# Windowed attention with a softplus feed-forward layer: the softmax weights of chunks 2 to 8 turned by VectorE in squares of 32 and a trip through DRAM

## The chip, the cores and the metric

The kernel runs on one core of one Trainium2 chip. The metric is the device time of one execution in microseconds, as the median of several runs; smaller is better.

## The reference

Eight batches of 576 tokens with eight heads of 64 go through causal attention in a window. Heads 0 to 3 see the last 32 keys, heads 4 to 7 see 32 keys with a step of four. The result, 4608 tokens by 512, goes through a feed-forward layer with softplus:

```python
scores = scale * np.matmul(q, k.transpose(0, 1, 3, 2))
scores = np.where(masks[None, :, :, :], scores, -1000000000.0)
scores = scores - np.max(scores, axis=-1, keepdims=True)
attn = np.exp(scores)
attn = attn / (np.sum(attn, axis=-1, keepdims=True) + 1e-09)
x = matmul(attn, v), heads side by side      # 4608 x 512
h = x @ w_in                                 # 4608 x 2048
g = np.maximum(h, 0.0) + np.log1p(np.exp(-np.abs(h)))
out = g @ w_out                              # 4608 x 512
```

Everything is float32; products are made of high and low parts on TensorE, three matmuls for one.

## The kernel before

The 4608 tokens are cut into nine chunks of 512. Chunks 0 and 1 are opened by an order written out by hand and go through the feed-forward layer first, by 32 slots of one feed-forward tile each. For chunks 2 to 8 (`FIRST` is 2) the first product, x times w_in, is made by seven products of half size in place of eight. That is the main loop at the end of the program: for each chunk eight pairs p of feed-forward tiles, and for each pair seven steps k. A step is `product` (six matmuls of 128x256 into one of two PSUM banks, `h_x` or `h_y`), `aside` (VectorE takes the bank out to `temps` or `hs`, L799 and L801), and then one output part, or two after the seventh step (`outputs`, `late_o`: three matmuls of 128x512 into `o_ps`). The banks alternate, so a product can start only when the bank that was filled two products before has been taken out. After steps 6 and 7 come the softplus of two tiles (three ACT passes L512 to L514, DVE L519, ACT L534, DVE L540).

The attention of a later chunk is spread over this loop by a list of events with due times, counted in feed-forward tiles; `pump(now)` after each step runs whatever is due. For each chunk there are four groups (`Group`, two heads each), and `attend(c, j, when, unit)` gives a group three events:

- `scores` at `when`: 32 matmuls of 64x96 into two banks `s_ps` (`score`), scale and mask on VectorE (L345, twice), the row maximum (L348), eight exponentials on ScalarE (L354), the sum's inverse (L366, L369), and the division of all 128x768 weights `s` on GpSimd (L372). Right after it the q and k of the next group are loaded.
- `turn` two tiles later: sixteen TensorE transposes of 64x96 to 96x64 into two banks `t_ps` (L394) and two ScalarE copies of 96x512 to `pt` (L407), so that keys lie on partitions.
- `values` 0.6 tiles after that: 32 matmuls `a_ps` of `v` with `pt`, and a ScalarE copy to `x_full` (L442), which later feeds the sums and splits of the next chunk's half-size products.

`s_ps`, `t_ps` and `a_ps` share two PSUM banks (`att`). In chunks 2 to 8 there is one buffer each for `s`, `pt`, `k` and `v`, and two for `q`. SyncE's queue issues all loads in the order of the events; w_out tiles (`t<-w_out`) are loaded three tiles ahead. TensorE instructions and transfers by `load_dma` are pinned to program order; much of VectorE's work is placed by the framework's scheduler.

Of the kernel before, what the change touches and what calls it, by code (L numbers as in the profile page):

```python
# [13 lines left out]
F32 = mybir.dt.float32  # L14
# [9 lines left out]
P = 128  # L24
# [5 lines left out]
BLK = 64  # L30
WKEYS = BLK + WIN
NB = CH // BLK
NS = NB // 2
# [8 lines left out]
FIRST = 2  # L42
HALF = CH // 2
NPAIR = NFF // 2
EARLY = 6
ON_POOL = 5
NEG = -1.0e9
# [42 lines left out]
def tile_windowed_attention_softplus_ffn(  # L90
# [11 lines left out]
    nc = tc.nc  # L102

    const = ctx.enter_context(tc.tile_pool(name="const", bufs=1))
    wk = ctx.enter_context(tc.tile_pool(name="wk", bufs=2))
    dpool = ctx.enter_context(tc.tile_pool(name="dec", bufs=3))
    psum = ctx.enter_context(tc.tile_pool(name="psum", bufs=2, space=bass.MemoryType.PSUM))
# [3 lines left out]
    slots, at = [], {0: 0, 1: 0}  # L111
# [12 lines left out]
    def pin(ins):  # L124

        if opening:
            tc.keep_in_program_order(ins)

    def load_dma(engine=None, **kw):
        tc.keep_in_program_order((engine or nc.sync).dma_start(**kw))  # L130
# [55 lines left out]
    def matmul(**kw):  # L186
        tc.keep_in_program_order(nc.tensor.matmul(**kw))  # L187

    def bank(name, tag="att"):
        return psum.tile(  # L190
            [P, CH], F32, name=name, tag=tag, bufs=2 if tag in ("att", "h") else 1
        )
# [8 lines left out]
    def scratch(shape, name, c, pr):  # L201

        if c == 0:
            tag = idle.pop(0)
        elif c == 1:
            tag = turns[name][pr % len(turns[name])]
        else:
            tag = f"q{pr % 2}" if name == "q" else name
        return const.tile(shape, F32, name=name, tag=tag)

    masks, xt = {}, {}
# [11 lines left out]
    def x_tiles(c):  # L223

        if c not in xt:
            xt[c] = [
                [const.tile([P, 2, CH], F32R, name=n, tag=f"{n}{c}{k}") for k in range(2)]
                for n in ("xh", "xl")
            ]
        return xt[c]  # L230
# [3 lines left out]
    def x_half(c, k):  # L234
        if (c, k) not in x_full:
            x_full[c, k] = const.tile([P, 2, CH], F32, name="x_full", tag=f"x_{'ab'[k]}")
        return x_full[c, k]
# [20 lines left out]
    def split(c, name):  # L258
        if name not in blocks:
            blocks[name] = const.tile(  # L260
                [P, 2, 2, HALF], F32R, name=name, tag=HOMES[ORDER.index(name)]
            )
        dst, n = blocks[name], int(name[1:])
        if name[0] == "a":
            src = x_block(c, n // 10 - 1, n % 10 - 1)
        else:
            src = combined[c, (n - 1) // 2][:, (n - 1) % 2]
        nc.scalar.copy(out=dst[:, 0], in_=src)
        nc.vector.tensor_tensor(out=dst[:, 1], in0=src, in1=dst[:, 0].bitcast(F32), op=ALU.subtract)

    class Group:
# [6 lines left out]
        def load_k(self, engine=None):  # L278
            kw = DKW if self.dil else PKW
            self.k = scratch([P, kw], "k", self.c, self.pr)  # L280
            src = kdl[self.c, self.pr - 2] if self.dil else kpl[self.c, self.pr]
            load_dma(engine, out=self.k, in_=src)

        def load_q(self):
            self.q = scratch([P, CH], "q", self.c, self.pr)
            load_dma(out=self.q, in_=qp[self.c, self.pr])
# [5 lines left out]
        def load_v(self):  # L292
            self.v = scratch([P, NB, 2, D], "v", self.c, self.pr)
            load_dma(out=self.v[:WKEYS], in_=vp[self.c, self.pr])
# [91 lines left out]
        def transposes(self):  # L386
# [12 lines left out]
                        )  # L399
            self.pt = scratch([P, 2, CH], "pt", self.c, self.pr)  # L400

        def turned(self, g):
            dst, src = self.pt[:WKEYS, g], self.banks[g][:WKEYS]
            if self.own and g:
                pin(nc.vector.tensor_copy(out=dst, in_=src))
            else:
                pin(nc.scalar.copy(out=dst, in_=src))  # L407

        def turn(self):
            self.transposes()  # L410
            self.turned(0)
            self.turned(1)

        def weighted(self):
            a_ps = bank("a_ps", "o2" if self.own else "att")
            by_class = a_ps.rearrange("p (r i) -> p r i", r=DIL)
            per = BLK // DIL
            for i in range(NS):
                for g in range(2):
                    n = 2 * i + g  # L420
                    for r in range(2):
                        rows = slice(r * D, (r + 1) * D)
                        if self.dil:
                            dst = a_ps[rows, n * BLK : (n + 1) * BLK]
                        else:
                            dst = by_class[rows, :, n * per : (n + 1) * per]
                        matmul(
                            out=dst,
                            lhsT=self.v[:WKEYS, n, r, :],
                            rhs=self.pt[:WKEYS, g, (r * NS + i) * BLK : (r * NS + i + 1) * BLK],  # L430
                            start=True,
                            stop=True,
                        )
            if self.c >= FIRST:
                self.x = x_half(self.c, self.pr // 2)[:, self.pr % 2], None, a_ps
                return
            xh, xl = x_tiles(self.c)
            self.x = *(part[self.pr // 2][:, self.pr % 2] for part in (xh, xl)), a_ps
# [15 lines left out]
    groups = [Group(c, pr) for c in range(NCH) for pr in range(NPR)]  # L454
# [24 lines left out]
    def at(when, part, *what):  # L479
        events.append((when, len(events), part, what))  # L480

    def attend(c, j, when, unit):
        n = c * NPR + j
        at(when, scores, n)
        at(when + 2 * unit, turn, n)
        at(when + 2.6 * unit, values, n)

    def pump(now):
        while events and events[0][0] <= now:
# [50 lines left out]
        pin(nc.vector.tensor_tensor(out=gl, in0=e, in1=gh.bitcast(F32), op=ALU.subtract))  # L540
        ready[i] = gh, gl

    dram = ctx.enter_context(tc.tile_pool(name="dram", bufs=1, space=bass.MemoryType.DRAM))
    kept = dram.tile([2, NKT, P, CH], F32, name="kept")
    w_out = dram.tile([NFF, P, 2, DM], F32, name="w_out")
    o_ps = {}
# [91 lines left out]
    for word in OPENING.split():  # L638
        name = word[:3] if word[0] == "D" and word[1] != "l" else word.rstrip("0123456789_")
# [15 lines left out]
    def weight_sum(p, j):  # L655

        parts = wt[2 * p + j, 0].bitcast(F32)
        if p < EARLY:
            sums[p, j] = dpool.tile([P, 2, HALF], F32, name="b", tag="a")
# [8 lines left out]
    def weight_13(p):  # L668
        shape = dict(shape=[P, 2, HALF], dtype=F32, name="t")
        d = diffs[p] = dpool.tile(**shape, tag="a") if p < EARLY else const.tile(**shape, tag="x_d")  # L670
        one, two = sums[p, 0], sums[p, 1]
# [16 lines left out]
    def second(p):  # L688

        q = min(p, NPAIR - 2)  # L690
        return [rests[q][:, p - q, part] for part in range(2)]

    def weight_split_24(p):
        if p < NPAIR - 1:
            rests[p] = const.tile([P, 2, 2, HALF], F32R, name="t2", tag=f"w{2 * p + 1}_1")
        parted(*second(p), sums[p, 1][:, 1])
        b12 = wt[2 * p + 1, 0]
        parted(b12[:, 0, :HALF], b12[:, 1, :HALF], sums[p, 0][:, 1])
# [44 lines left out]
    for ff in range(NFF):  # L743
        at(17.2 + 0.5 * ff, keep_w_out, ff)
    for j in range(NPR):
        attend(FIRST, j, 12 + 3.6 * j, 1)
    for n in range(4):
        at(26 + 0.2 * n, combine, FIRST, n)
    for k in range(4):
        at(27.6 + 0.4 * k, split, FIRST, ORDER[k])  # L750
    for p in range(NPAIR):
        at(20.5 + 1.9 * p if p < EARLY else 36.5 + 3 * (p - EARLY), convert, p)
    for c in range(FIRST + 1, NCH):
        base = 2 * NFF + (c - 1 - FIRST) * NFF
        for j in range(NPR):
            attend(c, j, base + 3.5 * j + (0.6 if c == FIRST + 1 else -0.4), 1)
        for n in range(4):
            at(base + 13.7 + 0.1 * n, combine, c, n)
    events.sort(key=lambda e: e[:2])
# [43 lines left out]
    def late_softplus(u):  # L803
        i = len(slots) + u
        tiles[i] = hs.pop(u)
        activated(i)
        softplus(i)
        g_high(i)
        g_low(i)
# [52 lines left out]
    between = {0: (1, 1, 1, 1, 0, 1, 1), 1: (1, 1, 0, 0, 1, 1, 2)}  # L862
    for n, (c, p) in enumerate((c, p) for c in range(FIRST, NCH) for p in range(NPAIR)):
        u = 2 * n
        for k, (x, weights, b, first, to, temp) in enumerate(steps):
# [5 lines left out]
            if k > 4:  # L871
                late_softplus(u + k - 5)
            if p == NPAIR - 1 and c + 1 < NCH:
                split(c + 1, x)
# [6 lines left out]
    for half in range(2):  # L881
        ob = const.tile([P, NKT, HALF], F32, name="pt", tag=("pt", "v")[half])
        for m in range(NKT):
# [9 lines left out]
            elif m % 2:  # L893
                nc.sync.dma_start(
                    out=out[(m - 1) * P : (m + 1) * P, cols].rearrange("(m p) n -> p m n", p=P),
                    in_=ob[:, m - 1 : m + 1],
# [116 lines left out]
```

## Time and profile before

| | us |
|---|---|
| median of 3 runs | 918.48 |
| lowest and highest run | 916.78, 920.76 |
| the profiled execution's own time | 918.32 |
| span in its profile | 916.5 |
| TensorE busy | 897.8 (98%) |
| VectorE busy | 610.8 (67%) |
| ScalarE busy | 574.1 (63%) |
| GpSimd busy | 62.6 (7%) |

The span is the time from the first to the last instruction of the profiled execution; 1.8 us of its time lie around it. An engine's share is an average over stages, and a matmul's listed duration is longer than the distance to the next one, because matmuls overlap in the array. So the cost of a block of matmuls is read from the distance of the starts around it and not from its durations. The granted TensorE clock is 0.996 of full speed over the span.

### The profile page before, as it was taken

To read this page: it belongs to the slowest core of one execution; us is meant where nothing else is said; L and a number is where in the kernel's file an instruction comes from. 1 tells how busy PE (TensorE), PEld (TensorE's weight loads), DVE (VectorE), ACT (ScalarE), POOL (GpSimd) and SP (SyncE) were. 2 spreads that over 40 slices of the span, in tenths; PEclk is the share of its full clock that TensorE was granted. 3 is DMA by queue.
4 is the path that set the end of the run, shared out by engine and by line. 5 is a ranking of instruction groups with operands and counts; after the bars stand their busy time and mean duration, and the time that the engine had idled before them with its cause. 6 is when DMAs were issued, how large, how long until landed. Compare 5 with 4: busy or idle time off the path is not lost.

```text
span 916.5 us, 19113 instructions
## 1 busy us (share of the span) xinstructions
PE 897.8 (98%) x7426; PEld 756.9 (83%) x7426; DVE 610.8 (67%) x1214; ACT 574.1 (63%) x1404; POOL 62.6 (7%) x46
## 2 busy tenths in 40 slices
PE   7899999999999999999999999999999999999998
PEld 4567877778878888888888888888888888898987
DVE  3899995997685575557655665557556765575444
ACT  5676687776565676666666576567655766654443
POOL 1320000000001000000000000000000000000000
PEclk8999999999999999999999999999999999999999
DMA  9979323225234335343443344333534353324323
GB/s 291 312 244 398 130 87 129 85 81 161 96 122 135 125 125 182 136 137 115 167 150 135 107 148 164 129 134 117 175 136 135 121 176 118 110 93 144 109 93 116
DMA packets 62971, 134.45 MB, mean 147 GB/s; under 512 B 7072, under 2 KB 9248, under 8 KB 62880
## 3 DMA queue, kind: packets, MB, share of 16 engines
q1 hardware_dynamic: 62304, 132.15, 41.8%
q8 instruction: 59, 0.97, 0.4%
q10 hardware_dynamic: 576, 1.07, 0.4%
q14 instruction: 32, 0.26, 0.1%
HBM read 113.27 MB, written 19.92 MB: 145 GB/s over the span
## 4 chain that ended last, share of the span: by engine, by line
PE 87%; DVE 8%; ACT 2%; DMA 1%; issue 1%; POOL 0%; ACTq 0%; DVEq 0%; POOLq 0%
PE o_ps L187 40%; PE h_x L187 18%; PE h_y L187 14%; PE h_ps L187 6%; PE a_ps L187 4%; PE s_ps L187 3%; PE t_ps L394 2%; ACT s L354 1%; DVE a L160 1%; DVE a L165 1%; DVE a L151 1%; DMA k<-kpl 1%; DVE e L519 1%; DVE a L155 1%; DVE gl L540 1%
## 5 line engine op out<-in xcount | busy, mean ns | idle before, releaser
L187 PE MATMUL o_ps<-gh,t 128*128 128x512 f32 (+1 forms) x904 | 341.6, 391 | 0.0
L187 PEld LDWEIGHTS o_ps<-gh,t 128*128 128x128 f32 x904 | 169.7, 188 | 21.3
L187 PE MATMUL o_ps<-gl,t 128*128 128x512 f32 (+1 forms) x452 | 178.2, 394 | 0.3 <-DVE gl L540 0.3
L512 ACT ACTIVATE e<-hs 128x512 f32<-128x512 f32 x112 | 69.1, 627 | 88.8 <-DVE hs L801 87.7
L354 ACT ACTIVATE s<-s,nm 128x96 f32<-128x96 f32 x224 | 80.9, 363 | 65.8 <-DVE nm L348 65.4
L519 DVE SCALAR_TENSOR_TENSOR e<-hs,e 128x512 f32<-128x512 f32 x112 | 79.5, 711 | 54.7 <-ACT e L514 54.7
L534 ACT CAST gh<-e 128x512 fp32r<-128x512 f32 x134 | 82.5, 617 | 42.7 <-DVE e L519 37.8
L540 DVE TENSOR_TENSOR gl<-e,gh 128x512 fp32r<-128x512 f32 x144 | 98.5, 694 | 9.1 <-ACT gh L534 8.8
L372 POOL TENSOR_TENSOR s<-s,ri 128x768 f32<-128x768 f32 x36 | 55.3, 1535 | 720.2 <-DVE ri L369 312.2
L187 PEld LDWEIGHTS h_x<-a,parts 128*128 128x128 f32 x672 | 94.7, 189 | 11.2 <-DVE hs L801 2.0
L187 PE MATMUL h_y<-s,t 128*128 128x256 f32 x672 | 101.6, 287 | 0.5 <-DVE temps L801 0.5
L187 PEld LDWEIGHTS h_y<-s,t 128*128 128x128 f32 x672 | 92.2, 188 | 10.7 <-DVE temps L801 0.9
L187 PE MATMUL h_x<-a,parts 128*128 128x256 f32 x672 | 98.5, 282 | 0.0
L801 DVE TENSOR_TENSOR hs<-h_x,temps 128x256 f32<-128x256 f32 x112 | 47.3, 422 | 66.4 <-PE h_x L187 66.0
L513 ACT ACTIVATE e<-e 128x512 f32<-128x512 f32 x144 | 88.8, 626 | 2.3
L514 ACT ACTIVATE e<-e 128x512 f32<-128x512 f32 x144 | 88.9, 626 | 2.1
L187 PEld LDWEIGHTS o_ps<-gl,t 128*128 128x128 f32 x452 | 86.0, 190 | 3.7 <-DVE gl L540 0.9
L187 PE MATMUL o_ps<-gh,parts 128*128 128x512 f32 x256 | 88.1, 395 | 0.0
L187 PE MATMUL h_ps<-xh,parts 128*128 128x512 f32 x256 | 87.0, 396 | 1.1 <-ACT xh L442 1.1
L801 DVE TENSOR_TENSOR temps<-h_y,temps 128x256 f32<-128x256 f32 x112 | 47.2, 422 | 25.7 <-PE h_y L187 23.8
L187 PEld LDWEIGHTS h_ps<-xh,parts 128*128 128x128 f32 x256 | 48.0, 188 | 12.4 <-ACT xh L442 1.6
L187 PEld LDWEIGHTS o_ps<-gh,parts 128*128 128x128 f32 x256 | 48.1, 188 | 10.4
(80 smaller groups left out, 1291.5 us busy)
## 6 DMA issues: line engine op xcount, KB each, us to landing
t<-w_out SPq DMA_DIRECT2D x224, 256.0 KB, 2.9
raw<-w SPq DMA_DIRECT2D x32, 512.0 KB, 10.2
v<-vp SPq DMA_DIRECT2D x36, 384.0 KB, 3.4
q<-qp SPq DMA_DIRECT2D x36, 256.0 KB, 3.8
w_out<-parts SPq DMA_DIRECT2D x16, 512.0 KB, 3.2
out_t<-ob SPq DMA_DIRECT2D x32, 256.0 KB, 2.1
k<-kdl SPq DMA_DIRECT2D x17, 320.0 KB, 4.0
k<-kpl SPq DMA_DIRECT2D x16, 272.0 KB, 3.2
```

What stands on the lines that cost most here:

```text
L151: pin(nc.vector.tensor_scalar(out=a, in0=a, scalar1=W_MIN, scalar2=W_MAX, op0=ALU.max, op1=ALU.min))
L187: tc.keep_in_program_order(nc.tensor.matmul(**kw))
L354: pin(nc.scalar.activation(out=self.blocks[:, t], in_=src, func=AF.Exp, bias=self.nm[:, t : t + 1], scale=1.0 / 8.0 if self.masked else 1. ...
L372: pin(nc.gpsimd.tensor_tensor(out=self.blocks, in0=self.blocks, in1=self.ri.unsqueeze(2).to_broadcast([P, NB, WKEYS]), op=ALU.mult,))
L394: nc.tensor.transpose(out=banks[g][:WKEYS, (r * NS + i) * BLK : (r * NS + i + 1) * BLK], in_=self.s[rows, k0 : k0 + WKEYS], identity=ident ...
L512: pin(nc.scalar.activation(out=e, in_=tiles[i], func=AF.Abs))
L513: pin(nc.scalar.activation(out=e, in_=e, func=AF.Exp, scale=-1.0))
L514: pin(nc.scalar.activation(out=e, in_=e, func=AF.Ln, bias=1.0))
L519: pin(nc.vector.scalar_tensor_tensor(out=e, in0=tiles.pop(i), scalar=0.0, in1=e, op0=ALU.max, op1=ALU.add))
L534: nc.scalar.copy(out=gh, in_=ready[i])
L540: pin(nc.vector.tensor_tensor(out=gl, in0=e, in1=gh.bitcast(F32), op=ALU.subtract))
L801: nc.vector.tensor_tensor(out=dst, in0=src, in1=temps[:, temp], op=ALU.add)
```

## The change

For chunks 2 to 8 the sixteen transposes and two copies of a group go. In their place VectorE turns `s` in one instruction, each square of 32x32 within its 32 partitions (`turn_squares`); the result (128x768, buffer `q1`) is written to DRAM in one transfer (`send_squares`), and three transfers, one for each 32 keys, read it back into `pt` (`fetch_squares`), 1 KB runs, 128 for each transfer. `values` reads `pt` in two runs of 32. The three of `attend` become five events: scores, turn, send, bring, values. Scores of chunks 4 to 8 are due 1.1 tiles earlier than before, and values 4.5 tiles after their scores in place of 2.6; since scores are 3.5 tiles apart, values now stand behind the scores of the next group. `q` has one buffer (`q0`) in these chunks, since `q1` holds the squares.

```diff
+        def turn_squares(self):
+
+            squares = const.tile([P, WKEYS // SQ, NB, SQ], F32, name="squares", tag="q1")
+            nc.vector.transpose(out=squares, in_=self.blocks.rearrange("p t (b k) -> p b t k", k=SQ))
+            self.squares = squares
+
+        def send_squares(self):
+            self.sent = dram.tile([P, WKEYS // SQ, NB * SQ], F32, name="turned", bufs=2)
+            load_dma(out=self.sent, in_=self.squares.rearrange("p b t n -> p b (t n)"))
+
+        def fetch_squares(self):
+            self.pt = scratch([P, P // SQ, NB, SQ], "pt", self.c, self.pr)
+            for b in range(WKEYS // SQ):
+                load_dma(
+                    out=self.pt[b * SQ : (b + 1) * SQ].rearrange("k q t n -> k q (t n)"),
+                    in_=self.sent[:, b].rearrange("(q k) n -> k q n", k=SQ),
+                )
+
+        def weights_of(self, g, t):
+            if self.c >= FIRST:
+                return self.pt[:WKEYS, 2 * g : 2 * g + 2, t]
+            return self.pt[:WKEYS, g, t * BLK : (t + 1) * BLK]
...
         def turn(self):
+            if self.c >= FIRST:
+                self.turn_squares()
+                return
             self.transposes()
...
-    def attend(c, j, when, unit):
+    def attend(c, j, when, lags):
         n = c * NPR + j
-        at(when, scores, n)
-        at(when + 2 * unit, turn, n)
-        at(when + 2.6 * unit, values, n)
+        for lag, part in zip((0,) + lags, (scores, turn, send, bring, values)):
+            at(when + lag, part, n)
...
-        attend(FIRST, j, 12 + 3.6 * j, 1)
+        attend(FIRST, j, 10.8 + 3.5 * j, (0.5, 2.8, 3.2, 4.5))
...
-            attend(c, j, base + 3.5 * j + (0.6 if c == FIRST + 1 else -0.4), 1)
+            attend(c, j, base + (3.73 * j - 2.1 if c == FIRST + 1 else 3.5 * j - 1.5), (0.5, 2.25, 2.65, 4.5))
```

TensorE, program before: a group's turn, in a stretch of the main loop (`h_x` and `h_y` are products, `o_ps` output parts).

```order
L187 MATMUL h_y<-a_2771,parts 128x256 x6
L187 MATMUL o_ps_2992<-gh,t_2604 128x512
L187 MATMUL o_ps_2992<-gl,t_2604 128x512
L187 MATMUL o_ps_2992<-gh,t_2695 128x512
L394 MATMUL t_ps<-consts,s 96x64 x16
L187 MATMUL h_x<-s_2774,parts 128x256 x6
```

In the changed program (its line numbers are two higher here, 32 higher in the main loop) no row of TensorE has `t_ps` in chunks 2 to 8, and product follows output part directly at these places.

VectorE, program before: the turn from one chunk to the next, where the finished output tiles are copied to `ob`.

```order
L801 TENSOR_TENSOR hs<-h_x,temps 128x256
L519 SCALAR_TENSOR_TENSOR e<-hs,e 128x512
L799 COPY temps<-h_x 128x256
L835 COPY ob<-o_ps_4220 128x512
L540 TENSOR_TENSOR gl<-e,gh 128x512
L519 SCALAR_TENSOR_TENSOR e<-hs,e 128x512
L801 TENSOR_TENSOR temps<-h_y,temps 128x256
L540 TENSOR_TENSOR gl<-e,gh 128x512
L799 COPY hs<-h_x 128x256
L835 COPY ob<-o_ps_4222 128x512
L801 TENSOR_TENSOR temps<-h_y,temps 128x256
L345 SCALAR_TENSOR_TENSOR s<-s_ps,mask 128x384 x2
```

VectorE, changed program, the same turn:

```order
L833 TENSOR_TENSOR hs<-h_x,temps 128x256
L552 SCALAR_TENSOR_TENSOR e<-hs,e 128x512 x2
L347 SCALAR_TENSOR_TENSOR s<-s_ps,mask 128x384 x2
L573 TENSOR_TENSOR gl<-e,gh 128x512
L831 COPY temps<-h_x 128x256
L573 TENSOR_TENSOR gl<-e,gh 128x512
L867 COPY ob<-o_ps_4105 128x512
L350 TENSOR_REDUCE nm<-s 128x8
L833 TENSOR_TENSOR temps<-h_y,temps 128x256
L831 COPY hs<-h_x 128x256
```

The scores of the chunk's second group now stand right behind step 7 of the first pair, so their mask, one `gl`, and later the maximum and a copy to `ob` have come ahead of the first two bank copies of the next pair. This order stands at five turns (the second groups of chunks 4 to 8).

SyncE's queue, changed program, one group's transfers among the loads of w_out:

```order
L132 DMA turned<-squares 128x768
L132 DMA t_2552<-w_out 128x512
L132 DMA t_2683<-w_out 128x512
L132 DMA pt<-turned 32x4x256 x3
L132 DMA t_2069<-w_out 128x512
L132 DMA t_2247<-w_out 128x512
L132 DMA q<-qp 128x512
```

Before, this queue held only loads here; the write and the three reads are new, each with its own place among them.

## Rows read from the trace of the kernel before

**Rows 1.** Busy time by stage: us, then busy us of each engine, clock, DMA share, GB/s.

```profile
100.00:200.00 100.00, 99.10 (x675) 79.47 (x674) 88.15 (x168) 75.75 (x178) 6.47 (x4) 1.00 0.27 98
400.00:520.00 120.00, 120.00 (x1059) 104.34 (x1059) 73.73 (x150) 73.66 (x184) 7.35 (x5) 1.00 0.41 138
```

**Rows 2.** Waits of TensorE: who waited for whom, us in total, times, longest.

```profile
PE t_ps L394 <- POOL s L372: 0.9, 1, 0.9
...
PE h_x L187 <- DVE hs L799: 0.7, 1, 0.7
```

**Rows 3.** Instructions on the tile t_ps: duration in ns, min, median, max.

```profile
L394 PE MATMUL t_ps<-consts,s x576: 216/216/340, 15.2 to 798.5; 64*96 64x64 f32 x192
L407 ACT COPY pt<-t_ps x68: 558/583/607, 18.6 to 799.2; 96x512 f32<-96x512 f32 x68
```

**Rows 4.** Timeline of TensorE around one turn: start us, duration us.

```profile
318.37 0.40 PE L187 MATMUL o_ps<-gh,t 128*128 128x512 f32 x1
...
319.16 0.65 PE L394 MATMUL t_ps<-consts,s 64*96 64x64 f32 x16
319.75 0.98 PE L187 MATMUL h_x<-s,t 128*128 128x256 f32 x6
320.56 0.40 PE L187 MATMUL o_ps<-gh,t 128*128 128x512 f32 x1
...
321.26 0.87 PE L187 MATMUL h_y<-a,parts 128*128 128x256 f32 x6
321.97 0.40 PE L187 MATMUL o_ps<-gh,t 128*128 128x512 f32 x1
```

**Rows 5.** Groups of VectorE instructions by shape: busy us, mean ns.

```profile
L348 DVE TENSOR_REDUCE nm<-s 128x8 f32<-128x768 f32 x28 | 26.4, 943 | 0.0
...
L155 DVE TENSOR_SCALAR a<-a 128x512 int32<-128x512 int32 x32 | 14.3, 456 | 0.3
...
L366 DVE TENSOR_SCALAR sm<-sm 128x8 f32<-128x8 f32 x36 | 6.0, 167 | 15.3 <-ACT s L354 15.3
```

**Rows 6.** Timeline of all engines around one group's scores.

```profile
396.39 0.87 PE L187 MATMUL h_x<-s,parts 128*128 128x256 f32 x6
...
397.29 0.42 DVE L801 TENSOR_TENSOR hs<-h_x,temps 128x256 f32<-128x256 f32 x1 [0.97 <-PE h_x L187]
...
398.94 0.69 DVE L519 SCALAR_TENSOR_TENSOR e<-hs,e 128x512 f32<-128x512 f32 x1 [1.22 <-ACT e L514]
...
399.98 0.89 PE L187 MATMUL s_ps<-k,q 64*64 64x96 f32 x32
...
400.12 0.69 DVE L519 SCALAR_TENSOR_TENSOR e<-hs,e 128x512 f32<-128x512 f32 x1 [0.16 <-ACT e L514]
400.73 0.68 DVE L540 TENSOR_TENSOR gl<-e,gh 128x512 fp32r<-128x512 f32 x1
...
400.80 0.98 PE L187 MATMUL h_y<-s,t 128*128 128x256 f32 x6
...
401.33 1.02 DVE L345 SCALAR_TENSOR_TENSOR s<-s_ps,mask 128x384 f32<-128x384 f32 x2
...
401.62 0.39 PE L187 MATMUL o_ps<-gh,t 128*128 128x512 f32 x1
...
402.26 0.68 DVE L540 TENSOR_TENSOR gl<-e,gh 128x512 fp32r<-128x512 f32 x1
...
402.86 0.42 DVE L801 TENSOR_TENSOR temps<-h_y,temps 128x256 f32<-128x256 f32 x1
...
403.19 0.94 DVE L348 TENSOR_REDUCE nm<-s 128x8 f32<-128x768 f32 x1
...
404.05 0.41 DVE L799 COPY hs<-h_x 128x256 f32<-128x256 f32 x1
...
408.12 1.47 POOL L372 TENSOR_TENSOR s<-s,ri 128x768 f32<-128x768 f32 x1 [21.04 <-DVE ri L369]
```

**Rows 7.** Transfers: KB each, median us from issue to landing.

```profile
v<-vp SPq DMA_DIRECT2D x36, 384.0 KB, 3.4
...
w_out<-parts SPq DMA_DIRECT2D x16, 512.0 KB, 3.2
```

More of the change, by code (lines that the diff above doesn't have):

```diff
@@ L44 @@
 NPAIR = NFF // 2
+SQ = 32
 EARLY = 6
@@ L104, in tile_windowed_attention_softplus_ffn @@
     const = ctx.enter_context(tc.tile_pool(name="const", bufs=1))
+    dram = ctx.enter_context(tc.tile_pool(name="dram", bufs=1, space=bass.MemoryType.DRAM))
     wk = ctx.enter_context(tc.tile_pool(name="wk", bufs=2))
@@ L207, in scratch @@
         else:
-            tag = f"q{pr % 2}" if name == "q" else name
+            tag = "q0" if name == "q" else name
         return const.tile(shape, F32, name=name, tag=tag)
@@ L429, in weighted @@
                             lhsT=self.v[:WKEYS, n, r, :],
-                            rhs=self.pt[:WKEYS, g, (r * NS + i) * BLK : (r * NS + i + 1) * BLK],
+                            rhs=self.weights_of(g, r * NS + i),
                             start=True,
@@ L480, in at, with send, bring @@
         events.append((when, len(events), part, what))
-    def attend(c, j, when, unit):
+    def send(n):
+        groups[n].send_squares()
+    def bring(n):
+        groups[n].fetch_squares()
+    def attend(c, j, when, lags):
         n = c * NPR + j
-        at(when, scores, n)
-        at(when + 2 * unit, turn, n)
-        at(when + 2.6 * unit, values, n)
+        for lag, part in zip((0,) + lags, (scores, turn, send, bring, values)):
+            at(when + lag, part, n)
     def pump(now):
@@ L541, in g_low @@
         ready[i] = gh, gl
-    dram = ctx.enter_context(tc.tile_pool(name="dram", bufs=1, space=bass.MemoryType.DRAM))
     kept = dram.tile([2, NKT, P, CH], F32, name="kept")
```

## The prediction

> **What bounds the kernel now.** I read the table by stage first. [...] The loop is a TensorE loop with spare time on every other engine, but the spare time before each single hand-over is small, and that is where this change must be read. The stage of chunk 2's attention (100 to 200 us) is tighter: TensorE 99, VectorE 88 of 100 [rows 1].
>
> **What goes.** 576 transposes in sixteens are 36 groups [rows 3]; eight belong to chunks 0 and 1 and stay, 28 go. A duration of 216 ns each is no cost, since they overlap. The cost is read from starts [rows 4]. Without a block, a product follows the start of an output part after 0.70 us (320.56 to 321.26) and the next output part follows after 0.71 (to 321.97). With the block the same distances are 1.38 (318.37 to 319.75) and 0.81 (to 320.56). So a block costs 0.68 + 0.10 = 0.78 us, and 28 of them 21.8 us, all on the path. One turn also waits 0.9 us for the division [rows 2]; TensorE no longer waits for the division itself, so I count that as gone too. The two ScalarE copies of 0.58 us per group [rows 3] go as well, 1.16 us for each group on an engine that nothing in the loop waits for: nothing in the sum.
>
> [...]
>
> **What VectorE gets.** One turning of 128x768 per group. The trace has no such operation. From below: a one-input pass over 512 elements takes 0.456 us [rows 5], so 768 take 0.68. From above: 24 squares, each paid like the smallest VectorE instruction, 0.167 us [rows 5], make 4.0 us. I take 0.94 us, the maximum over the same 128x768 [rows 5], nearest in shape and size. That is 26 us more work over some 800, on an engine with 46 of 120 us free: no cost by its sum. Two things could make it one.
>
> First, it waits for GpSimd's division, and VectorE runs in order: what stands behind it waits too. In the order, the turning stands behind the inverse with one to four other instructions between, and a bank copy next. The division starts 8.1 us after the scores and ends after 9.6 [rows 6], so the turning ends at 10.6. A bank copy has spare time: from the end of one product to the start of the next into the same bank lie an output part, a product and an output part, 0.70 + 0.71 + 0.70 = 2.1 us [rows 4], and the copy takes 0.42 [rows 6], so it may come 1.7 us late. One copy is let through ahead of the turning, the next product ends 1.4 us later; so a block of about 2.6 us (division and turning) uses up 1.2 of the 1.7. I count nothing for these waits.
>
> Second, the order of VectorE has moved at the turn of a chunk, and there I count a wait. I work it out with starts from rows 6, zero being the start of the scores. Step 7's product starts 0.71 + 2 x 0.70 + 0.09 = 2.20 us before (0.09 is what a small block waits at its start, 319.16 against 318.37 + 0.70 [rows 4]). In rows 6 such a product, at 396.39, with its copy at 397.29, is followed by the two `e` at 398.94 and 400.12, so 2.55 and 3.73 us later; here at 0.35 and 1.53. Then, each start from the distance in rows 6: mask x2 at 2.14 (0.61 later), `gl` at 3.07 (0.93), the first bank copy at 3.67 (0.60), done at 4.09. The products on TensorE: 0.82 the first (399.98 to 400.80), its output part at 1.64, the second product at 2.34, the third due at 3.75. It needs that bank: it waits 0.34, to 4.09. VectorE goes on: `gl` at 4.00 (0.33 after the copy's start), `ob` at 4.60, the maximum at 5.20, the second bank copy at 6.06 (0.86), done at 6.48; the fourth product was due at 4.09 + 1.41 = 5.50 and waits 0.98. Together 1.3 us at each turn, five turns: 6.6 us. Before, the first of these copies stood ahead of the second `e` and there was no such wait.
>
> **What the queues get.** Four transfers per group. The write of 384 KB is priced between nothing hidden and the 3.2 us of a write of 512 KB, the three reads of 128 KB each by the 3.4 us of one read of 384 KB [rows 7]. The write is due 2.25 tiles after the scores, some 13.5 us at 6 us per tile (two tiles are seven products and eight output parts, 7 x 0.71 + 8 x 0.70 = 10.6 us, and with the small blocks some 12), when the turning has ended at 10.6. Landed at 16.7, read back at 20.1. Between scores and values stand 15 products, 18 output parts, one block of values and one of scores: 15 x 0.71 + 18 x 0.70 + about 2 = 25.3 us. So some 5 us are spare. Loads of w_out queue behind the write's landing for up to 3 us; they are issued two tiles (some 12 us) before use. With one `q` buffer, q is loaded after its scores, as k is already: some 20 us before use. Nothing for these. `values` behind the next scores moves blocks on TensorE, and adds none.
>
> **The sum.** Against the profiled execution's 918.3 us (0.2 below the median of the runs): 918.3 - 21.8 - 0.9 + 6.6 = 902.2; I say 902.
>
> **Rivals.**
> - *The turns cost nothing.* If the scheduler's order is kept but ScalarE, with 1.16 us less per group, delivers `e` earlier, the bank copies are in time: 902 - 6.6 = 895.6. For it: hardly a wait of this kind in before [rows 2]. Against it: the mask and one `gl` stand ahead of the copy whatever ScalarE does.
> - *More waits of the kind.* Chunk 2's stage has VectorE at 88 of 100 [rows 1], and four turnings more there; and if the 1.2 us used of 1.7 in the main loop is really 2.0, each group pays 0.3: 28 x 0.3 = 8.4, so 910.
> - *Slower than before: the turning itself is long.* It holds VectorE; the product after it ends on average 0.7 us into it, and its copy may be 1.7 us late, so a turning of T makes TensorE wait T - 2.4. At 4.0 us that is 1.6 x 28 = 45 us: 947. The gain of 16 us is eaten from 0.57 us per group on, T about 3.0 us. [...] Against it: every VectorE pass over 128 partitions in the trace runs at about 1 us per 768 elements.
> - *The round trip is late, so the change does not hide what it says.* TensorE stands at `values` in order; each microsecond beyond the spare 5 costs 28 us, so a trip of 8 us more than counted gives 902 + 84 = 986. The first microsecond beyond would already undo the gain. Against it: 3.2 and 3.4 us are what transfers of this size take now [rows 7], at a DMA share of 0.41 [rows 1]. [...]
>
> **How the numbers follow.** Forecast (turns wait about as counted, 898 to 907) 0.45; turns free, about 896, 0.25; more waits, about 910, 0.20; long turning 0.06; late round trip 0.04. No change means within 0.5%, 4.6 us, of 918.5, about what a measurement here can tell. The first two are faster, 0.70, and of the third 0.18: 0.88. The third's rest (0.02) and two thirds of the long turning (T near 3) are the same: 0.06. The rest, 0.06, is slower. The range takes in the two neighbours of the forecast, 894 (turns free and a wait or two less) to 914; the two mishaps stay out.
>
> **What would show it.** In the changed profile: no `t_ps` after 90 us; 28 turnings of about 0.94 us, each ending some 11 us after its scores; TensorE's waits for bank copies (`temps`, `hs`) at about 7 us, in five pairs of 0.3 and 1.0 some 95 us apart; `values` waiting for no transfer. The forecast is wrong if a turning takes over 2 us, if TensorE waits for `pt`, or if chunk 2's stage has new waits.

## The result and the profile after

The changed kernel takes 907.08 us (median of 4 runs, 906.36 to 907.80) against 918.38 (4 runs, 916.78 to 920.76): a ratio of 0.9875, 95% interval 0.9852 to 0.9898. It is faster, within the forecast range (894 to 914), by 11.3 us where 16 were forecast. Its profiled execution took 907.07 us, span 905.3.

The table by stage, after (columns as in [rows 1]):

```profile
100.00:200.00 100.00, 98.86 (x624) 80.02 (x623) 95.76 (x178) 74.78 (x178) 6.56 (x4) 1.00 0.37 131
400.00:520.00 120.00, 118.95 (x987) 103.02 (x986) 78.98 (x157) 69.18 (x168) 6.13 (x4) 1.00 0.53 173
```

The reader sees two things against [rows 1]. In the main loop TensorE now has 1 us of holes in 120 where it had none. In chunk 2's stage VectorE has gone from 88 to 96 of 100 us: it is full.

The new operations, by tile (duration in ns: min, median, max), and their transfers, from the page (KB each, median us from issue to landing):

```profile
L407 DVE STREAM_TRANSPOSE squares<-s x28: 962/966/979, 123.2 to 776.8; 128x768 f32<-128x768 f32 x28
```

```profile
turned<-squares SPq DMA_DIRECT2D x28, 384.0 KB, 3.8
pt<-turned SPq DMA_DIRECT2D x84, 128.0 KB, 2.7
```

All as forecast: 0.966 us for a turning (0.94 taken), 3.8 + 2.7 us for the trip (3.2 + 3.4 taken). TensorE's waits, from their list (who for whom, us in total, times, longest), are where the rest went:

```profile
PE h_y L189 <- DVE temps L833: 3.8, 6, 0.7
...
PE h_x L189 <- DVE temps L831: 1.3, 5, 0.3
PE h_x L189 <- DVE hs L833: 1.1, 2, 0.7
PE h_ps L189 <- DVE e L552: 1.1, 1, 1.1
...
PE o_ps L189 <- DVE gl L573: 1.0, 1, 1.0
```

The wait for GpSimd of [rows 2] is gone, there is none for a transfer into `pt`, and bank copies (`temps`, `hs`) are waited for 13 times in these rows. Here is one turn of a chunk, TensorE first (start us, duration us, at the end the idle time before and for whom):

```profile
328.55 0.39 PE L189 MATMUL o_ps<-gh,t 128*128 128x512 f32 x1
328.99 0.98 PE L189 MATMUL h_y<-a,parts 128*128 128x256 f32 x6
329.81 0.40 PE L189 MATMUL o_ps<-gh,t 128*128 128x512 f32 x1
...
346.77 0.39 PE L189 MATMUL o_ps<-gh,t 128*128 128x512 f32 x1
347.42 0.98 PE L189 MATMUL h_x<-a,parts 128*128 128x256 f32 x6 [0.25 <-DVE temps L831]
348.23 0.40 PE L189 MATMUL o_ps<-gh,t 128*128 128x512 f32 x1
...
348.70 0.39 PE L189 MATMUL o_ps<-gh,t 128*128 128x512 f32 x1
349.81 0.98 PE L189 MATMUL h_y<-s,t 128*128 128x256 f32 x6 [0.72 <-DVE temps L833]
350.62 0.40 PE L189 MATMUL o_ps<-gh,t 128*128 128x512 f32 x1
```

and VectorE in the same stretch:

```profile
345.41 1.01 DVE L347 SCALAR_TENSOR_TENSOR s<-s_ps,mask 128x384 f32<-128x384 f32 x2
346.34 0.68 DVE L573 TENSOR_TENSOR gl<-e,gh 128x512 fp32r<-128x512 f32 x1
346.94 0.42 DVE L831 COPY temps<-h_x 128x256 f32<-128x256 f32 x1
347.28 0.68 DVE L573 TENSOR_TENSOR gl<-e,gh 128x512 fp32r<-128x512 f32 x1
347.88 0.68 DVE L867 COPY ob<-o_ps 128x512 f32<-128x512 f32 x1
348.48 0.94 DVE L350 TENSOR_REDUCE nm<-s 128x8 f32<-128x768 f32 x1
349.34 0.41 DVE L833 TENSOR_TENSOR temps<-h_y,temps 128x256 f32<-128x256 f32 x1
```

This is the row of work that the forecast wrote out: masks, `gl`, copy, `gl`, `ob`, maximum, copy. The product at 347.42 starts as the first copy is done, that at 349.81 as the second is. Without a wait a product follows the start of the last matmul of an output part after 0.23 us, and the next output part follows it after 0.71. Here the first distances are 0.44, 0.65 and 1.11, and each time the second is 0.81 or 0.82: a wait costs 0.1 more at the restart. So the three cost 0.3, 0.5 and 1.0 us. The same three stand at all five turns. Of the pair at 347 and 349 the forecast had 0.34 and 0.98; the third, 18 us earlier and not in the list, it did not have.

The period of a chunk shows it without any single wait. The first copy to `ob` of two chunks, before and after:

```profile
350.53 0.69 DVE L835 COPY ob<-o_ps 128x512 f32<-128x512 f32 x1 [0.27 <-PE o_ps L187]
447.17 0.69 DVE L835 COPY ob<-o_ps 128x512 f32<-128x512 f32 x1 [0.27 <-PE o_ps L187]
```

```profile
347.88 0.68 DVE L867 COPY ob<-o_ps 128x512 f32<-128x512 f32 x1
443.31 0.68 DVE L867 COPY ob<-o_ps 128x512 f32<-128x512 f32 x1
```

96.64 us before, 95.43 after: 1.21 less, where four blocks of 0.78 are 3.12. So a turn costs 1.9, not 1.3.

The account, profile against profile: the opening to the first copy to `ob`, which the change does not touch, took 93.6 us before and 92.0 after (92.0 to 94.8 in the profiles of this study, so a single profile is not better known than that). From there to the first half-size product, the stage of chunk 2's attention, it was 146.3 and should have been 142.3 (four blocks and the division's 0.9 less); it is 144.5, 2.2 more than forecast. The five turns cost 5 x 0.6 = 3 more than forecast, and chunk 3's stage some 1.3. -1.6 + 2.2 + 3 + 1.3 = 4.9: from 902.2 to 907.1.

Of the 2.2 us, 0.9 is not a loss. The matmuls on `s_ps` between the first copy to `ob` and the first half-size product, before and after (columns as in [rows 1], without GpSimd; TensorE's first):

```profile
93.61:239.95 146.34, 3.56 (x128) 2.81 (x128) 4.06 (x8) 0.00 (x0) 1.00 0.32 110
```

```profile
92.00:236.50 144.50, 4.45 (x160) 3.51 (x160) 5.07 (x10) 0.00 (x0) 1.00 0.38 132
```

Four groups' scores stood there before, five now: the scores of chunk 3's first group are due 2.7 tiles earlier in the changed kernel (the description of the change names only chunks 4 to 8), and have come over from chunk 3's stage. A group's scores cost TensorE 0.9 us by the starts around them (a product follows an output part's last matmul after 1.14 us, 342.94 to 344.08, and after 0.23 without them). So chunk 2's stage lost 1.3 us, which is the wait of 1.1 for `e` with its restart, and chunk 3's stage, which has become 0.9 lighter, lost 2.2.

### The profile page after: what moved, and what is told of

It reads as the page before. It is cut to its first block, busy times and chain, and to the rows that moved or that the text cites. A ratio compares the mean times of both kernels' runs of the same rounds, so it can differ in the third digit from the quotient of the medians.

```text
span 905.3 us, 18339 instructions
## 1 busy us (share of the span) xinstructions
PE 879.8 (97%) x6972; PEld 742.3 (82%) x6978; DVE 634.9 (70%) x1242; ACT 542.0 (60%) x1348; POOL 64.1 (7%) x46
## 4 chain that ended last, share of the span: by engine, by line
PE 79%; DVE 12%; ACT 5%; DMA 2%; issue 2%; ACTq 0%; SPq 0%; DVEq 0%
PE o_ps L189 37%; PE h_x L189 17%; PE h_y L189 12%; PE h_ps L189 7%; PE a_ps L189 3%; ACT s L356 2%; PE s_ps L189 2%; DVE e L552 1%; DVE gl L573 1%; DVE s L347 1%; ACT e L547 1%; DMA k<-kpl 1%; DVE nm L350 1%; DMA out_t<-ob 1%; DVE a L162 1%
## 5 line engine op out<-in xcount | busy, mean ns | idle before, releaser
L552 DVE SCALAR_TENSOR_TENSOR e<-hs,e 128x512 f32<-128x512 f32 x112 | 76.4, 686 | 49.6 <-ACT e L547 49.5
L189 PEld LDWEIGHTS h_y<-s,t 128*128 128x128 f32 x672 | 94.6, 188 | 15.7 <-DVE temps L833 5.7
L189 PEld LDWEIGHTS h_x<-a,parts 128*128 128x128 f32 x672 | 92.5, 189 | 16.0 <-DVE hs L833 3.8
L189 PE MATMUL h_x<-a,parts 128*128 128x256 f32 x672 | 101.4, 287 | 2.6 <-DVE temps L831 1.3
L189 PE MATMUL h_y<-s,t 128*128 128x256 f32 x672 | 98.5, 282 | 3.8 <-DVE temps L833 3.6
```

The source lines that it names most:

```text
L552: pin(nc.vector.scalar_tensor_tensor(out=e, in0=tiles.pop(i), scalar=0.0, in1=e, op0=ALU.max, op1=ALU.add))
```

## The experiments

The theory after the result (A): the blocks are gone at their price, the turning and the trip cost nothing by themselves, and what was lost is VectorE's order, at the turns and where VectorE is full. The rival (B): the loss belongs to the turning itself or to the trip.

**The second group's scores one step earlier.**

```diff
-            attend(c, j, base + (3.73 * j - 2.1 if c == FIRST + 1 else 3.5 * j - 1.5), (0.5, 2.25, 2.65, 4.5))
+            attend(c, j, base + (3.73 * j - 2.1 if c == FIRST + 1 else 3.5 * j - 1.5 - 0.3 * (j == 1)), (0.5, 2.25, 2.65, 4.5))
```

> Only the second group's scores of chunks 4 to 8 (and what follows from them) are due 0.3 tiles earlier, one step ahead of the two output parts at the end of a pair in place of behind them. Theory A (the three waits of TensorE at each chunk's turn, 0.3 + 0.5 + 1.0 us, come from where these scores stand: mask, gl and maximum get ahead of two bank copies): the waits of 0.5 and 1.0 go at all five turns, 7.5 us, to about 899.5; the small one of 0.3 may stay. Theory B (VectorE has too much work in these stretches with the turning added, wherever the scores stand): the waits move by a step or two and stay near 1.5 us a turn, 907.

901.9 us (900.93 to 902.63), ratio 0.9825 (0.9811 to 0.9838). VectorE at the same place:

```profile
344.99 0.94 DVE L350 TENSOR_REDUCE nm<-s 128x8 f32<-128x768 f32 x1
345.85 0.68 DVE L573 TENSOR_TENSOR gl<-e,gh 128x512 fp32r<-128x512 f32 x1
346.44 0.42 DVE L831 COPY temps<-h_x 128x256 f32<-128x256 f32 x1
346.84 0.69 DVE L867 COPY ob<-o_ps 128x512 f32<-128x512 f32 x1
347.55 0.42 DVE L833 TENSOR_TENSOR temps<-h_y,temps 128x256 f32<-128x256 f32 x1
```

The maximum now lies ahead of the next pair's first copy, with one `gl`, and between the first copy and the second stands only `ob`. Both waits are gone at all five turns; the third, 0.3 us, stays. The period of a chunk is 94.13, 1.30 less and not 1.5, because a new small wait has come (a product at 377.06 starts 0.32 behind the last matmul of an output part in place of 0.23, with its restart 0.2 us, at all five chunks). This confirms A for the turns. 899.5 was not reached: five chunks of 1.30 are 6.5 of the expected 7.5, and the opening, which the edit does not touch, took 93.1 us in this profile and 92.0 in that of the changed kernel.

**No turning at all.** What is written to DRAM is `s` itself, in a view of the same shape; this leaves out the turning. The trip stays.

```diff
-            squares = const.tile([P, WKEYS // SQ, NB, SQ], F32, name="squares", tag="q1")
-            nc.vector.transpose(out=squares, in_=self.blocks.rearrange("p t (b k) -> p b t k", k=SQ))
-            self.squares = squares
+            self.squares = self.s.rearrange("p (b t n) -> p b t n", b=WKEYS // SQ, n=SQ)
```

> The turning on VectorE is left out: the transfers write the unturned weights to DRAM, and all else stands as in the change, so the values are products of wrong weights. Theory A (turn waits from the order): the five turns keep their 1.8 us each, and only the waits that stand beside a turning between 160 and 285 us go, some 4 us: about 903. Theory B (the turning is what VectorE cannot take): all new waits go, 12 us: about 895.

905.17 us (903.89 to 908.79), ratio 0.9867 (0.9849 to 0.9886). The period of a chunk is 95.36, with the same waits of 0.25 and 0.72 at the turns: the 20 turnings of chunks 4 to 8 cost next to nothing. Counted from the first copy to `ob`, the profile is 3.1 us shorter than that of the changed kernel (810.2 against 813.3), 0.9 of it before the first half-size product, where the wait of 1.1 for `e` is gone, and 1.8 in chunk 3's stage behind it. So the turning costs 2.7 us in the two stages where VectorE is full, most of the 1.3 and 2.2 that they lost. The medians are 1.9 us apart: less than A's 4, and far from B's 12.

**The removal alone.** The kernel before with `turn` returning at once in chunks 2 to 8; `values` there reads blocks of `s` as they are. It leaves out the transposes and their copies, and moves and adds nothing.

```diff
         def turn(self):
+            if self.c >= FIRST:
+                return
             self.transposes()
...
-                            rhs=self.pt[:WKEYS, g, (r * NS + i) * BLK : (r * NS + i + 1) * BLK],
+                            rhs=(
+                                self.s[:WKEYS, r * SW + i * WKEYS : r * SW + i * WKEYS + BLK]
+                                if self.c >= FIRST
+                                else self.pt[:WKEYS, g, (r * NS + i) * BLK : (r * NS + i + 1) * BLK]
+                            ),
```

> The kernel before, in which the transposes and copies of chunks 2 to 8 are left out and nothing is put in their place; values multiply the unturned weights, and all due times are those of before. It prices what the change takes out. By 28 blocks of 0.78 us and the wait of 0.9: 918.4 - 22.7 = 895.7. A rival: if products next to the blocks hid part of them, or VectorE's bank copies come too late once TensorE is faster, less is gained, 900 or more.

897.88 us (895.73 to 902.42), ratio 0.9788 (0.9764 to 0.9812). The copies to `ob` stand 93.52 us apart (347.71 and 441.23), 3.12 less than before: four blocks of 0.78, the forecast's price to the hundredth, and TensorE waits for nothing in chunks 4 to 8. The run gained 20 us, where blocks and division come to 22.7. In the profiled execution (900.64) the rest was lost early. Chunk 2's stage has a new wait:

```profile
PE h_ps L187 <- DVE e L525: 0.9, 1, 0.9
```

and chunk 3's stage takes 97.6 us as before, though its waits are hardly longer in sum (1.8 us, before 1.5): behind one of them, of 1.47 us, TensorE's granted clock falls to 0.50, which the last section shows. So the expectation's rival, that less is gained because VectorE comes late once TensorE is faster, holds in these two stages, without any turning. Of this kernel's runs, the one at a mean clock of 0.998 took 895.73, the price; that at 0.986 took 902.42.

**The turning doubled.**

```diff
+            nc.vector.transpose(out=squares, in_=self.blocks.rearrange("p t (b k) -> p b t k", k=SQ))
             nc.vector.transpose(out=squares, in_=self.blocks.rearrange("p t (b k) -> p b t k", k=SQ))
```

> Each turning is made twice, the second with the same result, 0.97 us more of VectorE per group. Theory A (a turning fits into the spare time of the bank copies in the main loop, and costs only in the stretches up to 285 us): 3 to 6 us more, most of it before 285 us: 910 to 913. Theory B (VectorE is at its limit all through): TensorE waits 0.5 us or more for each of the 28, 14 us or more: 921 and up.

919.22 us (917.22 to 920.94), ratio 1.0009 (0.9996 to 1.0022): between the two expectations. TensorE's waits there:

```profile
PE h_ps L189 <- DVE e L553: 2.3, 1, 2.3
PE o_ps L189 <- DVE gl L574: 2.2, 6, 0.9
```

The wait for `gl` is new at each turn, the period of a chunk is 96.6 again, and chunks 2 and 3 lose more. One turning of 1 us fits into VectorE's spare time in the main loop, a second does not: the spare time was small, as [rows 4, 6] had let one expect, and the whole gain hung on it.

**The trip 3 and 6 us later** (chunks 3 to 8; with 2.75, 3.15 and with 3.25, 3.65):

```diff
-            attend(c, j, base + (3.73 * j - 2.1 if c == FIRST + 1 else 3.5 * j - 1.5), (0.5, 2.25, 2.65, 4.5))
+            attend(c, j, base + (3.73 * j - 2.1 if c == FIRST + 1 else 3.5 * j - 1.5), (0.5, 3.25, 3.65, 4.5))
```

> The changed kernel with the write to DRAM and the three reads of chunks 3 to 8 issued 0.5 tiles, about 3 us, later; the values stay where they are, and nothing else moves on TensorE. Theory A (the trip has some 4 us to spare in every group, as issue times and values in the changed kernel's trace say, and what it lost is VectorE's order): the same time, 907 within 1.5 us, and no wait of TensorE for pt. Theory B (the trip is the near limit, and the prediction's 5 us spare was too much): TensorE waits for pt, 0.5 to 2 us in each of 24 groups, 919 to 955.

> The same with 1.0 tiles, about 6 us, later. By the changed kernel's trace (reads landed 19 to 25 us after the scores' start, values from 26 to 29) the reads now land at 25 to 31, about 2 us behind the values on average: 24 x 2 = 48, so about 955. By the prediction's 5 us of spare time: 1 us late, 907 + 24 = 931. If it stays at 907, the trip had over 6 us to spare.

909.97 us (907.77 to 911.43), ratio 0.9909 (0.9892 to 0.9925), and 951.87 us (950.25 to 959.66), ratio 1.0382 (1.0351 to 1.0414). The line on `pt` in TensorE's list, for 3 us and for 6:

```profile
PE a_ps L189 <- DMA pt<-turned: 2.2, 2, 1.3
```

```profile
PE a_ps L189 <- DMA pt<-turned: 30.0, 18, 3.6
```

With 3 us, 22 of 24 groups wait for nothing and two do, 0.9 and 1.3 us; it is 1.5 us above what A allowed. With 6 us, 18 groups wait, 1.7 us on average. The delays do not reach all groups alike: with 3 us more, the write of chunk 5's third group goes out 16.1 us after its scores, as it did without, that of its fourth 18.5 in place of 13.6. So the spare time is better read in the changed kernel itself, from the landing of a group's last read to its first matmul on `pt`. It is 1.6 to 8.0 us in these 24 groups, 5.1 in the mean. The tightest is chunk 6's third group: its last read is issued at 579.0 and lands 2.8 us later at the latest, and its values start 1.6 after that.

```profile
L132 SPq DMA_DIRECT2D pt<-turned x3: 319/422/431, 578.2 to 579.0; - x3
DMA to landing us min/median/max: 2.5/2.6/2.8
583.51 1.15 PE L189 MATMUL a_ps<-pt,v 96*64 96x64 f32 x32
```

The forecast's 5 was the mean, and right in that nothing was late; but the third groups of chunks 5 to 7 had only 1.6 to 2.3 us.

**Both of a chunk's first two groups moved** (the first 0.3 tiles later, the second 0.3 earlier):

```diff
-            attend(c, j, base + (3.73 * j - 2.1 if c == FIRST + 1 else 3.5 * j - 1.5), (0.5, 2.25, 2.65, 4.5))
+            attend(c, j, base + (3.73 * j - 2.1 if c == FIRST + 1 else 3.5 * j - 1.5 + (0.3, -0.3, 0, 0)[j]), (0.5, 2.25, 2.65, 4.5))
```

> The changed kernel with the second group's scores 0.3 tiles earlier, as in the run before, and also the first group's scores 0.3 tiles later, in chunks 4 to 8. Theory A (all three waits at each turn of a chunk come from VectorE's order there; the smallest, 0.30 us before an h_y with its restart of 0.10, too): it goes at all five turns, 901.9 - 5 x 0.4 = 899.9, between 898.5 and 901. Theory B (the small wait has another cause, the next chunk's sums or ScalarE): it stays at all five turns and the time is 901.9 again, 901 to 903.

906.02 us (903.78 to 909.25), ratio 0.9868 (0.9847 to 0.9889): neither expectation was met. The small wait is gone, and at all five turns another has come, for `gl`:

```profile
PE o_ps L189 <- DVE gl L573: 2.9, 6, 1.0
```

The output part needs this `gl` at 341.2, and it is ready at 341.80. The first group's scores, moved by one step, took their turning with them:

```profile
338.39 0.96 DVE L407 STREAM_TRANSPOSE squares<-s 128x768 f32<-128x768 f32 x1
339.59 1.26 DVE L552 SCALAR_TENSOR_TENSOR e<-hs,e 128x512 f32<-128x512 f32 x2
```

ScalarE's passes of this softplus also run 1.3 us later than in the changed kernel, counted from the first product of the chunk. But the first of its results that `e` needs is there at 338.5, and `e` starts only at 339.59, behind the turning and a copy. So the last hold is VectorE's order once more; what ScalarE's delay adds is not shown.

**Chunk 2 turned by TensorE**, on the kernel with both groups moved; chunks 3 to 8 as in the change:

```diff
...
-            if self.c >= FIRST:
+            if self.c > FIRST:
                 self.turn_squares()
...
-        attend(FIRST, j, 10.8 + 3.5 * j, (0.5, 2.8, 3.2, 4.5))
+        attend(FIRST, j, 10.8 + 3.5 * j, (2.0, 2.8, 3.2, 4.5))
```

> The kernel with both scores moved, but chunk 2's four groups turned by TensorE and copied by ScalarE as before the change; nothing else. It adds 4 x 0.78 = 3.1 us of TensorE to a stage where VectorE was busy for 96 of 100 us, and takes four turnings (3.9 us) from VectorE. Theory A (VectorE's load in this stage ate most of what the removed blocks gave, some 2 of 3.1 us between 93 and 237 us, and more behind it): only 0 to 1.5 us slower than the kernel with both scores moved. Theory B (the early loss has nothing to do with the turnings): 3 to 4 us slower.

907.2 us (906.41 to 909.77), ratio 0.9884 (0.9864 to 0.9904): 1.2 above the kernel that it is made from, as A had it, but not by A's account. Profile against profile, it loses 2.6 of the 3.1 us between the first copy to `ob` and the first half-size product, and wins 0.9 back in chunk 3's stage. So turning these four groups on VectorE is worth some 1.7 of 3.1 us there. Another 1.1 us went in two late stages; why is open. The medians, whose intervals overlap, cannot tell it from nothing.

**Two early groups moved**, in three ways, on the kernel with the second scores earlier: chunk 2's third group by -0.6, +0.3 and +0.6 tiles, chunk 3's first by +0.3, +0.6 and +0.9. The first of them:

```diff
-        attend(FIRST, j, 10.8 + 3.5 * j, (0.5, 2.8, 3.2, 4.5))
+        attend(FIRST, j, 10.8 + 3.5 * j - 0.6 * (j == 2), (0.5, 2.8, 3.2, 4.5))
...
-            attend(c, j, base + (3.73 * j - 2.1 if c == FIRST + 1 else 3.5 * j - 1.5 - 0.3 * (j == 1)), (0.5, 2.25, 2.65, 4.5))
+            attend(c, j, base + (3.73 * j - 2.1 + 0.3 * (j == 0) if c == FIRST + 1 else 3.5 * j - 1.5 - 0.3 * (j == 1)), (0.5, 2.25, 2.65, 4.5))
```

> The kernel with the second scores earlier (901.9), and also chunk 2's third group 0.6 tiles earlier and chunk 3's first group 0.3 tiles later. In VectorE's order the turning of the one now stands behind an e, and that of the other behind the gl that TensorE waited for. Theory A (the 1.25 us wait at 165 us for e and the 1.16 us wait at 238 us for gl are there because a turning stands ahead of them in VectorE's queue): both are gone or under 0.3 us, and if nothing new comes the time is 901.9 - 2.2 = 899.7. Theory B (VectorE is simply full in these stages, 96 of 100 us): a wait of the same size shows elsewhere within a few us, and the time stays at 901 to 903.

> As the run before, but chunk 2's third group 0.3 tiles later and chunk 3's first group 0.6 tiles later: the gl stands ahead of chunk 3's first turning, but the turning of chunk 2's third group still stands four instructions ahead of an e. Theory A: the wait for gl at 238 us goes, the wait for e at 165 us stays, 901.9 - 1.1 = 900.8. Theory B: 901 to 903 with new waits.

> As the run before, but chunk 2's third group 0.6 tiles later and chunk 3's first group 0.9 tiles later: the e stands right ahead of the one turning, and the gl further ahead of the other. Theory A: both waits go, 899.7. Theory B: 901 to 903 with new waits of 1 us or more in the same stages.

901.33 us (ratio 0.9821, 0.9801 to 0.9841), 901.96 (0.9825, 0.9801 to 0.9848) and 905.49 (0.9863, 0.9837 to 0.9888), against 0.9825 without these moves. In the first, neither old wait is left, and two others have come:

```profile
219.83 0.50 PE L189 MATMUL o_ps<-gh,parts 128*128 128x512 f32 x1 [1.43 <-DVE ob L615]
...
241.38 0.98 PE L189 MATMUL h_y<-s,t 128*128 128x256 f32 x6 [1.76 <-DVE e L552]
```

B is right for the first two: with VectorE full, another order makes TensorE wait for another instruction, and the time stays. The third fits neither, 2.5 us above B's range. It has one wait of 2.00 us at 160.84 and this one:

```profile
243.91 0.80 PE L189 MATMUL h_y<-s,t 128*128 128x256 f32 x2 [2.48 <-DVE e L552]
```

Behind both TensorE's granted clock is down to 0.50 (162.0 to 165.4 and 244.0 to 247.2 us; more on this in the last section). So a moved due time moved the wait or made it longer, and none of the three wins the early loss back; that no order could is not shown. The best kernel of the study is the one with the second scores one step earlier, at 901.9 us, or its like with two early groups moved, at 901.33 or 901.96; they cannot be told apart.

## Why the prediction was right, and where it was 5 us off

- **What goes**: right. 0.78 us a block, read from the starts around one block [rows 4], is what the removal alone shows: 3.12 for four. The wait for the division went as well.
- **What VectorE gets**: 0.94 us was taken between 0.68 and 4.0; it is 0.966. The row nearest in shape, the maximum over the same 128x768 [rows 5], was the right one to take. As an estimate, the 0.966 is the smallest instruction's 0.167 [rows 5] and 1.04 ns for each of 768 elements. The 28 turnings took 962 to 979 ns, next to the 943 of the maximum over as many elements, and not 24 times 0.167. The rival of a long turning falls. Its counter-argument was misread, though: not every pass takes about 1 us per 768 elements, the 0.456 us over 512 that the forecast itself uses is 0.68.
- **"I count nothing for these waits"**: this step failed in part. It was right for chunks 4 to 8, where the chunk's period does not change without the turning (95.36 and 95.43). It was wrong for the stages of chunks 2 and 3, where VectorE had little room to begin with: 1.3 + 2.2 us by the account above, of which the run without turning gives 2.7 back. The rival "more waits" named chunk 2's stage and its 88 of 100, and should have been added to the sum, not kept as an alternative. The sign "new waits in chunk 2's stage" came true (1.1 us for `e`).
- **The wait at the turn**: right in place, number of turns and cause, mis-sized. 1.3 us was counted, 1.9 measured. Missing were the wait 18 us earlier, 0.3, and 0.2 at the first of the two in the list (0.34 counted, 0.42 and a restart of 0.1 measured); the last 0.1 is not accounted for. The forecast followed VectorE's order only at the place that it had chosen to show.
- **The trip**: right in the duration and in the mean of 5 us spare, but the mean was not what decides: the tightest group had 1.6. 3 us more and two groups are late. The loads of w_out did queue behind the write's landing: the reads ahead of them in SyncE's queue waited for it 21 times, 5.6 us at the longest, where up to 3 were taken; behind the opening TensorE waited for no transfer. The turning ended 9.3 to 12.6 us after its scores in chunks 4 to 8, where 10.6 was taken, and up to 15.5 in chunk 2.
- **ScalarE counts for nothing**: right here; in the changed kernel's list TensorE waits for ScalarE nowhere from 92 us on.
- **The opening**: 1.6 us of the forecast's nearness is no merit, since this profile's opening was by so much shorter. Without it the sum would have missed by 6.5; the range holds either way.
- The rivals: *turns free* is what the second scores one step earlier partly makes of it (901.9 and not 896, because 0.6 us a chunk and the early waits stay). *The round trip is late* begins with 3 us more, and with 6 it costs 45 us.

## What to carry to other kernels

Price a block on a full engine by the distance between the starts around it; that held to the hundredth here, while what its replacement cost was in VectorE's order and load. When work goes to an engine with spare time on average, look at each stage by itself, and count a wait where that engine is nearly full (88 of 100 us before, 96 after): there a shifted due time moved the wait or made it longer (three tries won nothing), while with spare time a single step earlier took out 1.3 us per chunk. When due times move, count what crosses from one stage into the next before calling a difference a loss. Read the spare time of a transfer in its tightest group, not in a typical one.

## What the runs showed that was not expected

After some waits of TensorE the granted clock falls to half (0.50 and 0.51 of full speed in the rows below). In the two cases below it does so when the engine has already resumed, some 2 us and some 1 us after. The long wait of the kernel with the removal alone, and the table by stage behind it (columns as in [rows 1]):

```profile
254.11 0.98 PE L187 MATMUL h_x<-s,t 128*128 128x256 f32 x6 [1.47 <-DVE hs L805]
```

```profile
254.50:258.00 3.50, 3.18 (x40) 2.49 (x39) 3.50 (x9) 1.65 (x3) 0.00 (x0) 0.75 0.07 22
258.00:263.00 5.00, 5.00 (x23) 4.47 (x20) 3.39 (x9) 2.87 (x6) 0.00 (x0) 0.50 0.27 79
263.00:268.00 5.00, 5.00 (x57) 4.10 (x56) 4.57 (x11) 3.55 (x8) 0.00 (x0) 0.99 0.54 175
```

TensorE is busy throughout from 258 to 263, but from a product's start to the next output part's it takes 1.28 us there, in place of 0.71:

```profile
260.93 1.48 PE L187 MATMUL h_x<-s,parts 128*128 128x256 f32 x6
262.21 0.63 PE L187 MATMUL o_ps<-gh,t 128*128 128x512 f32 x1
```

The kernel with the trip 6 us later shows it again, behind a wait of 3.60 us that ends at 403.46:

```profile
402.00:404.50 2.50, 1.04 (x32) 1.04 (x32) 0.00 (x0) 0.00 (x0) 0.18 (x1) 1.00 0.21 76
404.50:407.00 2.50, 2.50 (x13) 2.27 (x10) 0.77 (x2) 2.15 (x4) 0.00 (x0) 0.51 0.45 141
```

That kernel lost 44.8 us against the changed one with 30.0 us of waits for `pt`; its mean clock was 0.978, against 0.998. 0.020 of its 950 us is 19 us of clock, an estimate, enough for the 14.8 that the waits leave. In the changed kernel, whose waits behind the opening are at most 1.14 us, the clock stays at 1.00 from 92 to 895 us (0.96 over the rest). Not every long wait does it: the one of 1.76 us above was followed by no such stretch (1.00 from 241 to 250 us). In the kernel with the trip 6 us later one of 1.83 us, before the values at 357.67, was not followed by it either (1.00 from 358 to 365.5 us), while the shorter one of 1.47 in the kernel with the removal alone was. What decides was not tried. For this kernel it means that a long wait can cost more than its own length, as the 44.8 us for 30.0 of waits show.
